# Attention stage of a fused kernel: a warm-up on the identity, gates behind the first maxima, one turning for the factors, the last x^T multiplied by VectorE, another tie rule for the plan

## The chip, the cores and the metric

The kernel runs on one core of one Trainium2 chip. The metric is device time in microseconds (us) of one execution; a kernel's time is the median of its runs. The engines are named as the profile names them: PE is TensorE (PEld its weight loads), DVE is VectorE, ACT is ScalarE, POOL is GpSimd and SP is SyncE, which here only issues DMAs. Each engine works through its own instructions in program order and waits for the others by semaphores.

## The reference: what is computed

Three layers follow each other: attention with a compressive memory, an expert layer with one expert (`_moe_ref`), and a gated layer with eight experts (`_moe2_ref`). The change lies in the first one alone.

```python
# q, k, v: (4, 8, 576, 64); M_prev: (4, 8, 64, 64); z_prev: (4, 8, 64); beta: (8,)
scores = scale * np.matmul(q, k.transpose(0, 1, 3, 2))
scores = np.where(causal, -1000000000.0, scores)
scores = scores - scores.max(-1, keepdims=True)
a = np.exp(scores)
a /= a.sum(-1, keepdims=True) + 1e-09
local = np.matmul(a, v)
q_p = phi(q)                                   # phi(x) = max(x, exp(x) - 1) + 1 by pieces
mem_ret = np.einsum('bhsd,bhde->bhse', q_p, M_prev)
mem_norm = np.einsum('bhsd,bhd->bhs', q_p, z_prev)[..., None] + 1e-06
g = 1.0 / (1.0 + np.exp(-beta))[None, :, None, None]
attn_out = g * (mem_ret / mem_norm) + (1 - g) * local
```

The layer behind it multiplies each token by `w_in` (512 x 2048), applies an elementwise function, and multiplies by `w_out`; the last one routes each token to one of eight experts.

## The kernel before, in words

**Stages.** `fused_kernel` calls `attention` and then `moe`. Attention works on 16 pairs of heads (`NPAIR`); beside it the same engines already convert `w_in` to two parts (`cv`, 16 pieces) and, from pair 13 on, split the first two blocks of x^T (`xs`). `moe` begins on PE with `gemm1` (L197 to L199: products of x and `w_in` into PSUM tiles `ph`), and `gemm2` (L249 to L251: into `py`) follows three steps behind it. The parts of `w_out` are made in `moe` itself, step by step (L800, L808, L813, L819, L829, L832).

**One pair.** Per pair p, with its two heads side by side:

- SP loads `qk` (q^T and k^T), `qn` (q by rows) and `vx` (M_prev and v). POOL scales q^T (`sq`, L1009). ACT, DVE, POOL and DVE make phi(q) and its sums with z_prev (`f1` to `f4`, L1012 to L1027; `f3` is L1022 and L1024).
- PE makes the scores of query tiles 0 to 4 (`S0` makes tiles 0 and 1 together, then `S2`, `S3`, `S4`; L1041 to L1049) into two PSUM tiles `ps`. DVE takes their maxima (`pk`, L1055 and L1058), ACT the exponents with their sums (`ex`, L1069).
- POOL and DVE work out the factors in two parts (`s0`, `s1`, `s2`: L1081, L1085, L1090, L1091), and POOL writes phi(q) times a factor in front of the exponents in `E` (`place0`, `place1`, L1095), so that one product gives both the memory part and the local part.
- PE turns the blocks of `E` (L1101, at most four blocks of 128 columns to a PSUM tile `pt`, of which there are two); DVE or ACT copies each `pt` to `eta` or `etb` (L1001 on DVE, L1003 on ACT) and so frees it. `AV0` and `AV1` (L1129) multiply `vx` with `eta` and `etb` into the one PSUM tile `px`.
- The normalising factors `rr` of the pair are turned as well (`r`: L1107 twice and L1108 once, into a `pt`), copied to `rt` in two copies (`re`), stored to DRAM in two DMAs (`rw`, L1117 and L1118) and read back spread over 64 partitions for each head (`rs`, L1122, two DMAs) as `R`.
- `xe` copies `px` to `xt` (`xr` for the last pair) on DVE or ACT, `X` multiplies it by `R` on POOL (L1141), and `xo` stores it (L1145).

**What sets the order.** Everything in attention between the constants and `moe` is a task of `Work`: a name, an engine (or "VA": DVE or ACT, whichever starts first), an assumed duration, a due time, and the names it depends on. `run` repeatedly takes the task with the smallest rank among those whose dependences are placed, assumes when it starts and ends, and at last writes all tasks in the order of their assumed starts. No hardware queue is reordered by it: the order in which the code is written is the program order of each engine. The rank before:

```python
start = max(ready, free[e])
rank = (round((start + turn) * 8), t[0], t[1])     # t[0]: due time, t[1]: number
```

Starts are compared in steps of an eighth of a microsecond, and within a step the earlier due time wins.

**Start and end of the stage.** Before the plan, DVE clears 512 columns of `E[1]` (L1259) and PE makes two products of these zeros into `px` (`keep_warm`, L1257). The gates (sigmoid of beta and what follows from it: L979 on ACT, `gates1` with L982 to L991 on DVE) depend on nothing but `beta`. At the end, `moe`'s first `ph` takes the PSUM banks that `px` had, and the first parts of `w_out` take the SBUF space that attention's tiles had, `R` among them.

## Time and profile before

| What | Value |
|---|---|
| time, median of 3 runs | 908.55 us (906.96 to 911.33) |
| the profiled execution | 907.34 us |
| its span | 905.6 us |
| PE busy | 840.3 us (93%), 5412 products |
| DVE busy | 579.4 us (64%) |
| ACT busy | 622.4 us (69%) |
| POOL busy | 288.2 us (32%) |

Attention takes the span from its start to 236.6 us, where PE begins with `ph`. Busy time is an average over stages: the share of PE over the whole span says little of attention, so the rows below take stretches of their own. A row of the timeline gives start, duration, engine, line, operation, the tiles written and read, the number of merged instructions, and in brackets how long the engine had been idle and what ended that. A "wait" row gives who waited for whom, the sum, the number of times and the longest.

### The profile page before, as it was taken

The page shows a single profiled execution, that of the slowest core. Times are in us where ns is not written, and L with a number is a line of the kernel's source. Part 1 is how long each engine was busy: PE and PEld are TensorE (multiplying, and loading weights), DVE is VectorE, ACT ScalarE, POOL GpSimd, SP SyncE. Part 2 cuts the span into 40 slices and gives each one's busy share as a digit, 9 for nine tenths or more (in the row PEclk, how much of TensorE's full clock was granted, in tenths as well). Part 3 has the DMA queues.
Part 4 walks back from the last instruction along what each step waited for, and adds up shares of the span by engine and source line. Part 5 has one row for each costly group of instructions (what it writes and reads, how often), then busy time and mean ns, then how long its engine had stood idle before and what let it go on. Part 6 is the DMA issues. An engine that isn't in the chain of part 4 may idle for free. (4 is left out here: it accounts for less than half of the span.)

```text
span 905.6 us, 15113 instructions
## 1 busy us (share of the span) xinstructions
PE 840.3 (93%) x5412; PEld 684.3 (76%) x5412; DVE 579.4 (64%) x1166; ACT 622.4 (69%) x1136; POOL 288.2 (32%) x363
## 2 busy tenths in 40 slices
PE   6889889999889999999999999999878989999995
PEld 3556556666779998989898989888856868778774
DVE  6988888766478843456575757575457765383661
ACT  4777668876488887787878787787754555373551
POOL 5875877754223230110101111111055212211200
PEclk8999999999999999999999999999999999999998
DMA  5666566642333231010101010122326968284610
GB/s 211 197 189 195 181 195 222 210 154 86 123 94 109 94 128 48 24 47 24 48 24 48 25 47 24 47 96 92 105 79 222 363 205 286 61 281 163 202 57 4
DMA packets 53704, 113.44 MB, mean 125 GB/s; under 512 B 12148, under 2 KB 17396, under 8 KB 53600
## 3 DMA queue, kind: packets, MB, share of 16 engines
q1 hardware_dynamic: 43968, 91.22, 31.0%
q0 software_dynamic: 4064, 10.42, 3.5%
q10 hardware_dynamic: 5568, 10.49, 3.2%
q8 instruction: 56, 0.92, 0.4%
q14 instruction: 48, 0.39, 0.1%
HBM read 94.47 MB, written 18.77 MB: 125 GB/s over the span
## 5 line engine op out<-in xcount | busy, mean ns | idle before, releaser
L197 PE MATMUL ph<-xh,u 128*128 128x256 f32 x576 | 163.8, 284 | 0.9 <-DVE xr L1001 0.9
L199 PE MATMUL ph<-xh,u 128*128 128x256 f32 x576 | 162.5, 282 | 0.0
L198 PE MATMUL ph<-xl,u 128*128 128x256 f32 x576 | 162.3, 282 | 0.0
L249 PE MATMUL py<-u,gh 128*128 128x512 f32 x288 | 115.2, 400 | 5.4 <-POOL u L832 5.1
L251 PE MATMUL py<-u,gl 128*128 128x512 f32 x288 | 114.5, 398 | 1.4 <-DVE gl L235 1.4
L250 PE MATMUL py<-u,gh 128*128 128x512 f32 x288 | 114.4, 397 | 0.0
L197 PEld LDWEIGHTS ph<-xh,u 128*128 128x128 f32 x576 | 109.8, 191 | 3.4 <-DVE xr L1001 1.1
L198 PEld LDWEIGHTS ph<-xl,u 128*128 128x128 f32 x576 | 109.9, 191 | 2.5
L199 PEld LDWEIGHTS ph<-xh,u 128*128 128x128 f32 x576 | 109.9, 191 | 0.0
L225 DVE SCALAR_TENSOR_TENSOR g<-t,g 128x512 f32<-128x512 f32 x72 | 49.9, 693 | 92.4 <-ACT t L221 92.4
L1069 ACT ACTIVATE e<-ps,nm 128x256 f32<-128x256 f32 (+4 forms) x144 | 77.9, 550 | 28.9 <-DVE nm L1058 21.4
L235 DVE TENSOR_TENSOR gl<-g,gh 128x512 fp32r<-128x512 f32 x72 | 51.9, 721 | 69.0 <-ACT gh L234 59.2
L1101 PE MATMUL pt<-ident,e 128*128 128x128 f32 x528 | 76.2, 282 | 10.3 <-ACT eta L1003 4.6
L351 POOL DMA_INDIRECT rt<-pay,sl x18 | 20.7, 1148 | 187.6 <-DVE pay L349 184.9
L209 ACT ACTIVATE g<-ph 128x512 f32<-128x512 f32 x72 | 42.7, 593 | 49.4 <-PE ph L199 47.6
L1101 PEld LDWEIGHTS pt<-ident,e 128*128 128x128 f32 x528 | 56.6, 141 | 20.6 <-ACT eta L1003 6.4
L106 POOL TENSOR_TENSOR xl<-xr,xh 128x256 fp32r<-128x256 f32 x36 | 31.5, 880 | 112.0 <-ACT xh L105 111.8
L249 PEld LDWEIGHTS py<-u,gh 128*128 128x128 f32 x288 | 54.8, 190 | 16.0 <-POOL u L832 5.3
L251 PEld LDWEIGHTS py<-u,gl 128*128 128x128 f32 x288 | 54.4, 189 | 15.7 <-DVE gl L235 2.5
L832 POOL TENSOR_TENSOR u<-cvf,u 128x512 fp32r<-128x512 f32 x32 | 46.6, 1456 | 58.1 <-ACT u L829 58.1
L250 PEld LDWEIGHTS py<-u,gh 128*128 128x128 f32 x288 | 54.6, 189 | 9.8
L1058 DVE TENSOR_REDUCE nm<-ps 128x2 f32<-128x256 f32 (+1 forms) x64 | 51.3, 816 | 9.2 <-PE ps L1049 8.2
(238 smaller groups left out, 1987.3 us busy)
## 6 DMA issues: line engine op xcount, KB each, us to landing
raw<-w SPq DMA_DIRECT2D x25, 512.0 KB
qk<-qk SPq DMA_DIRECT2D x16, 608.0 KB
raw<-w_in SPq DMA_DIRECT2D x16, 512.0 KB
raw<-w_out SPq DMA_DIRECT2D x16, 512.0 KB
xl<-w SPq DMA_DIRECT2D x16, 512.0 KB
xh<-w SPq DMA_DIRECT2D x15, 512.0 KB
qn<-qn SPq DMA_DIRECT2D x16, 384.0 KB
vx<-vx SPq DMA_DIRECT2D x16, 320.0 KB
```

Of the source, the lines that this page charges most:

```text
L197: T.matmul(ps[:, f2], win(HI, k, f), hi[:, k], start=(k == 0), stop=False)
L198: T.matmul(ps[:, f2], win(HI, k, f), lo[:, k], start=False, stop=False)
L199: T.matmul(ps[:, f2], win(LO, k, f), hi[:, k], start=False, stop=(k == KD - 1))
L225: V.scalar_tensor_tensor(out=g, in0=t, scalar=ROOT_HALF, in1=g, op0=ALU.add, op1=ALU.mult)
L235: V.tensor_tensor(out=gl, in0=g, in1=gh.bitcast(F32), op=ALU.subtract)
L249: T.matmul(ys[i][t], gh[:, f2, ts], wout(HI, f), start=(f == 0), stop=False)
L250: T.matmul(ys[i][t], gh[:, f2, ts], wout(LO, f), start=False, stop=False)
L251: T.matmul(ys[i][t], gl[:, f2, ts], wout(HI, f), start=False, stop=(f == KF - 1))
L832: self.nc.gpsimd.tensor_tensor(out=lo, in0=self.now.pop(i), in1=hi.bitcast(F32), op=ALU.subtract)
L1058: V.tensor_reduce(out=nm, in_=ps[:, :, o:o + w], axis=AX.X, op=ALU.max, negate=True)
L1069: A.activation(out=E[p % 2][:, k, 64:64 + w], in_=src, func=AF.Exp, bias=nm[:, h:h + 1], scale=1.0, accum_out=SS[p % 2][:, 0, k:k + 1])
L1101: T.transpose(ps[:, c], E[p % 2][:, k, j * 128:(j + 1) * 128], ident)
```

## The change

Five edits, all in attention and in the planner:

- The warm-up products are twelve products of the identity with itself, 128 columns each, put ahead of the first loads; the two on zeros and the clearing for them are gone.
- The gates get due times and dependences: ACT's part waits for the first `f1`, DVE's part for the third maxima of pair 0 (`(0, "pk", 2)`, which are tile 2's). Two tasks stand for the loads of pair 0, so that the plan knows when they land; `load(0, "vx")` now comes first of the planned loads.
- The factors `rr` (nine columns) are turned by one transpose, copied by one copy and stored by one DMA. Reading them back takes four DMAs (per head one for the full tiles in pieces of 128 values, one for the 64 values of the last tile) in place of two. The due times of `r`, `re` and `rw` are 1.3 us, 1.3 us and 1.2 us earlier.
- The last pair's `px` is multiplied by `R` on DVE, straight from PSUM, in place of a copy on DVE and a product on POOL. It so depends on `rs` of that pair.
- The rank of the plan is the start plus a twentieth of the due time, unrounded.

```diff
-                        rank = (round((start + turn) * 8), t[0], t[1])
+                        rank = (start + turn + 0.05 * t[0], t[0], t[1])
...
+        for i in range(12):
+            T.matmul(px[:, 0, 0:128], ident, ident, start=True, stop=True)
         load(0, "qk")
         load(0, "qn")
...
         def turn_r(p):
             pts[p, "r"] = ps = ps_t.tile([128, 4, 128], F32, name="pt")
-            r = rrs.pop(p)[:, 0]
+            T.transpose(ps[0:NS, 0], rrs[p][:, 0], ident)
+
+        def keep_r(e, p):
+            evac(e, rt_, pts.pop((p, "r"))[0:NS, 0])
+
+        def store_r(p):
+            SP.dma_start(out=rd[p % 2], in_=rt_)
+
+        def spread_r(p):
+            d = rd[p % 2]
             for h in range(2):
-                T.transpose(ps[0:NQT, h], r[:, h:2 * NQT:2], ident)
-            T.transpose(ps[0:1, 2], r[:, 2 * NQT:NS], ident)
...
+                SP.dma_start(out=R[p % 2][HS[h], 0:QW].rearrange("p (t q) -> p t q", t=NQT),
+                             in_=d[0:2 * NQT].rearrange("(t h) (a q) -> h a t q", h=2, a=1)[h].to_broadcast([64, NQT, 128]))
+                SP.dma_start(out=R[p % 2][HS[h], QW:S], in_=d[2 * NQT:NS, HS[h]].to_broadcast([64, 64]))
...
-            evac(e, xt, pxf[:, 256:256 + S])
+            if p < NPAIR - 1:
+                evac(e, xt, pxf[:, 256:256 + S])
+            else:
+                V.tensor_tensor(out=xt, in0=pxf[:, 256:256 + S], in1=R[p % 2], op=ALU.mult)
...
-        wk.add(("lv0",), "S", 0.5, 0.5, lambda: load(0, "vx"), lag=3.5)
-        wk.add(("g0",), "A", 0.25, 4.0, gates0)
-        wk.add(("g1",), "V", 2.1, 5.0, gates1, [("g0",)])
+        wk.add((0, "lq"), "S", 0.5, -30.0, lambda: load(0, "vx"), lag=4.5)
+        wk.add((0, "ld"), "G", 0.1, -30.0, lambda: None, lag=4.0)
+        wk.add(("g0",), "A", 0.25, 4.0, gates0, [(0, "f1")])
+        wk.add(("g1",), "V", 3.0, 7.0, gates1, [("g0",), (0, "pk", 2)])
...
-            wk.add(key("r"), "T", 0.35, o + P + 3.3, lambda p=p: turn_r(p), [key("s2", 0), key("s2", 1)], take="t")
+            wk.add(key("r"), "T", 0.15, o + P + 2.0, lambda p=p: turn_r(p), [key("s2", 0), key("s2", 1)], take="t")
...
+            end = p == NPAIR - 1
+            wk.add(key("xe"), "V" if end else "VA", {"V": 0.7, "A": 0.6}, o + P + 8.0, lambda e, p=p: out_x(e, p),
+                   [key("AV0"), key("AV1")] + [("xs", 1, KD - 1), key("rs")] * end + [prev2("xo")])
...
-        V.memset(wtile[:, 0:512], 0.0)
-        for _ in range(2):
-            keep_warm()
         wk.run()
```

What that does to the order of the engines, at three places. The names in the rows: `nm` are negated maxima, `mn` is phi(q) on its way, `ss` are sums, `by` the gates by query tile; `eta`, `etb`, `pt`, `px`, `ps` as above.

DVE at the start of the stage, before (the last two copies, L990 and L991, come twice):

```order
L982 TENSOR_SCALAR gates<-gates 128x12
L983 RECIPROCAL gates<-gates 128x12
L984 TENSOR_SCALAR gates<-gates 128x12
L985 TENSOR_SCALAR gates<-gates 128x12
L986 RECIPROCAL gates<-gates 128x12
L987 TENSOR_TENSOR gates<-gates 128x12
L990 COPY by<-gates 128x4x2 x4
L991 COPY by<-gates 128x4
L1058 TENSOR_REDUCE nm_245<-ps 128x2
L1058 TENSOR_REDUCE nm_247<-ps 128x2
```

The same place on DVE with the change (its lines are two further down):

```order
L1019 SCALAR_TENSOR_TENSOR qn<-qn,mn_120 128x576
L1060 TENSOR_REDUCE nm_239<-ps 128x2
L1060 TENSOR_REDUCE nm_243<-ps 128x2
L1060 TENSOR_REDUCE nm_247<-ps 128x2
L1029 TENSOR_REDUCE ss_124<-mn_120 128x9
L984 TENSOR_SCALAR gates<-gates 128x12
L985 RECIPROCAL gates<-gates 128x12
L986 TENSOR_SCALAR gates<-gates 128x12
L987 TENSOR_SCALAR gates<-gates 128x12
L988 RECIPROCAL gates<-gates 128x12
L989 TENSOR_TENSOR gates<-gates 128x12
L992 COPY by<-gates 128x4x2 x4
```

The gates moved from ahead of the maxima of pair 0 to behind its first three maxima and `f4`; the fourth maxima (tile 3) come right behind them.

PE in the middle of the stage, around the turning of the factors of pair 7, before:

```order
L1101 MATMUL pt<-ident,e_114 128x128 x8
L1129 MATMUL px<-eta,vx 64x256 x2
L1129 MATMUL px<-eta,vx 64x192 x2
L1129 MATMUL px<-eta,vx 64x64 x2
L1101 MATMUL pt<-ident,e_114 128x128 x8
L1041 MATMUL ps<-qk 128x512
L1041 MATMUL ps<-qk 128x64
L1042 LDWEIGHTS idb
L1042 MATMUL ps<-m_138,idb 128x64
L1101 MATMUL pt<-ident,e_114 128x128 x3
L1107 MATMUL pt<-ident,rr 4x128 x2
L1108 MATMUL pt<-ident,rr 1x128
```

PE with the change, around the turning of the factors of pair 8:

```order
L1103 MATMUL pt<-ident,e_113 128x128 x8
L1127 MATMUL px<-eta,vx 64x256 x2
L1127 MATMUL px<-eta,vx 64x192 x2
L1127 MATMUL px<-eta,vx 64x64 x2
L1103 MATMUL pt<-ident,e_113 128x128 x4
L1107 MATMUL pt<-ident,rr 9x128
L1048 MATMUL ps<-qk 128x512 x2
```

The turning of the factors stood at the end of the pair's turnings; it now stands further ahead, in front of a score step. Over the whole stage, turnings of `E` with nothing but the factors' turning between them make 11 runs of 11 or more before and 3 with the change; the rest are runs of 8 or fewer.

PE at the passage from attention to `moe`, before:

```order
L1101 MATMUL pt<-ident,e_114 128x128 x15
L1107 MATMUL pt<-ident,rr 4x128 x2
L1108 MATMUL pt<-ident,rr 1x128
L1129 MATMUL px<-etb,vx 64x320 x6
L1129 MATMUL px<-etb,vx 64x256 x2
L1129 MATMUL px<-etb,vx 64x128 x2
L197 MATMUL ph<-xh,u_86 128x256
```

And with the change:

```order
L1103 MATMUL pt<-ident,e_114 128x128 x8
L1107 MATMUL pt<-ident,rr 9x128
L1103 MATMUL pt<-ident,e_114 128x128 x7
L1127 MATMUL px<-etb,vx 64x320 x6
L1127 MATMUL px<-etb,vx 64x256 x2
L1127 MATMUL px<-etb,vx 64x128 x2
L197 MATMUL ph<-xh,u_86 128x256
```

The last pair's factors are turned seven turnings earlier. From L197 on, PE's and SP's instructions are the same in both.

## Rows read from the trace of the kernel before

**Rows 1.** Three stretches: start and end, length, busy us (count) by engine, PEclk.

```profile
30.00:236.00 206.00, 186.75 (x1579) 125.08 (x1576) 164.62 (x274) 148.74 (x423) 138.16 (x210) 1.00 0.55 174
253.40:256.40 3.00, 2.94 (x7) 2.35 (x8) 2.93 (x4) 2.98 (x5) 1.64 (x1) 0.50 0.20 81
300.00:600.00 300.00, 299.38 (x1935) 269.22 (x1935) 174.66 (x470) 241.09 (x363) 45.15 (x45) 1.00 0.14 46
```

**Rows 2.** Waits of 30 to 236 us: who waited for whom, us, times, longest.

```profile
POOL xt L1141 <- DMA r<-rd: 22.3, 9, 5.4
...
PE pt L1107 <- DVE etb L1001: 5.5, 6, 1.2
...
PE pt L1101 <- ACT eta L1003: 4.3, 7, 1.6
...
PE pt L1101 <- POOL e L1095: 2.3, 2, 2.0
...
PE pt L1107 <- ACT etb L1003: 2.2, 2, 1.2
PE pt L1101 <- DVE etb L1001: 2.2, 3, 1.5
```

**Rows 3.** Timeline of the first 22 us: start, us, engine, line, operation, tiles.

```profile
1.10 0.29 POOL masks.py:199 TENSOR_SCALAR_AFFINE_SELECT ident<-ident 128x128 f32<-128x128 f32 x1
...
5.01 0.88 POOL L1009 TENSOR_SCALAR qk<-qk,nums,one 128x640 f32<-128x640 f32 x1 [1.04 <-DMA qk<-qk]
...
5.80 3.78 PE L1257 MATMUL px<-e 128*128 128x512 f32 x4 [5.80 <-DVE e L1259]
...
7.90 0.17 DVE L982 TENSOR_SCALAR gates<-gates 128x12 f32<-128x12 f32 x1
...
9.51 0.80 PE L1046 MATMUL ps<-qk 64*128 64x128 f32 x4
...
11.55 0.16 DVE L991 COPY by<-gates 128x4 f32<-128x4 f32 x1
11.62 1.01 DVE L1058 TENSOR_REDUCE nm<-ps 128x2 f32<-128x256 f32 x2
...
14.51 2.08 PE L1046 MATMUL ps<-qk 64*128 64x512 f32 x4 [2.42 <-DVE cvf L808]
...
18.81 1.72 POOL L1022 TENSOR_TENSOR mn<-qn 128x512 f32<-128x512 f32 x1 [1.65 <-DVE qn L1017]
...
19.08 1.12 PE L1101 MATMUL pt<-ident,e 128*128 128x128 f32 x4
...
21.22 0.21 POOL L1090 TENSOR_TENSOR rr<-rr,by 128x12 f32<-128x12 f32 x1
```

**Rows 4.** Groups of 30 to 225 us by shape: count, busy us, mean ns.

```profile
L1003 ACT ACTIVATE rt<-pt 4x256 f32<-4x256 f32 x11 | 4.0, 367 | 2.7 <-PE pt L1108 2.7
...
L1003 ACT ACTIVATE rt<-pt 1x128 f32<-1x128 f32 x11 | 2.8, 250 | 0.0
```

**Rows 5.** Timeline of the passage from attention to `moe`, 232 to 254 us.

```profile
232.83 0.38 PE L1107 MATMUL pt<-ident,rr 128*4 128x128 f32 x2 [0.58 <-DVE etb L1001]
...
233.35 0.61 DVE L1001 COPY rt<-pt 4x256 f32<-4x256 f32 x2 [0.30 <-PE pt L1108]
...
235.75 1.11 SPq L1122 DMA_DIRECT2D r<-rd  x2
235.78 0.76 DVE L1001 COPY xr<-px 128x576 f32<-128x576 f32 x1 [1.82 <-PE px L1129]
...
236.59 0.39 PE L197 MATMUL ph<-xh,u 128*128 128x256 f32 x1 [0.86 <-DVE xr L1001]
...
239.60 1.43 POOL L1141 TENSOR_TENSOR xr<-xr,r 128x576 f32<-128x576 f32 x1 [8.07 <-DMA r<-rd]
241.06 0.63 ACT L829 ACTIVATE u<-cvf 128x512 fp32r<-128x512 f32 x1 [7.04 <-POOL xr L1141]
...
253.45 0.76 PE L249 MATMUL py<-u,gh 128*128 128x512 f32 x1 [5.09 <-POOL u L832]
```

## The prediction, made before the change was run

> **What bounds the kernel now.** I read the stretches first. From 300 to 600 us PE is busy 299.38 us of 300 [rows 1]: behind attention the program is bound by PE's own products, and its order from the first `ph` on is unchanged. So a microsecond by which PE reaches `ph` earlier or later is a microsecond of the whole, and nothing else in the change can count. From 30 to 236 us PE is busy 186.75 us of 206, DVE 164.62, ACT 148.74 and POOL 138.16 [rows 1]: PE is the fullest engine of attention as well, but it stands idle for 19.25 us. The waits say for what: five rows of PE's waits add up to 5.5 + 4.3 + 2.3 + 2.2 + 2.2 = 16.5 us, and every one of them is a turning into `pt` (L1101, L1107) that waits for DVE or ACT to copy an earlier `pt` away, or for POOL to fill `E` [rows 2]. So attention has three prices to look at: PE's own work, these 16.5 us, and the start and the end of the stage, which I read from the timeline [rows 3, 5].

> The sum is made against the profiled execution, 907.34 us (span 905.6 and 1.74 around it). The median of the runs is 1.2 us above it.

> **Warm-up.** The first score product starts at 9.51, when the two products of zeros end (5.80 + 3.78 = 9.58); its operand has been ready since 5.01 + 0.88 = 5.89 [rows 3]. The identity is there at 1.10 + 0.29 = 1.39, so the twelve new products can start then. They are 24 instructions in the trace's way of counting, where two products of zeros were 4. Their price has two bounds. A quarter of a 512-column one: 3.78 / 4 / 4 = 0.236 us, 24 of them 5.7 us, ending at 7.1. Or a turning of 128 columns as at 19.08: 1.12 / 4 = 0.28 us, in all 6.7 us, ending at 8.1 [rows 3]. I take 7.4, near the first since it is the same kind of product: the scores start 2.1 us earlier (1.4 to 2.4, and 3.6 if the products ran so fast that the operand decides).

> **Gates.** DVE works on them from 7.90 to 11.55 + 0.16 = 11.71 and takes the first maxima at 11.62, though the first score block ended at 9.51 + 0.80 = 10.31 [rows 3]. Without that, and with scores 2.1 us earlier, the maxima can come at about 8.3, 3.3 us earlier, and so can ACT's exponents and the second PSUM tile, for which PE's next scores waited 2.42 us up to 14.51 [rows 3]. Not all of it stays: the same 3.81 us of gates now stand on DVE ahead of the fourth maxima, and behind those wait the fourth exponents and the reciprocal of pair 0. I count 2.5 us for warm-up and gates together (0 to 4).

> **Pair 0's factors.** On POOL, `f3` of pair 1 (L1022, 18.81 for 1.72 us, and its small second half) stood ahead of the factors of pair 0 (L1090 at 21.22) [rows 3]; with the change it comes behind them, so they can come up to 2.4 us earlier. `place0` and pair 0's turnings hang on them; behind them other copies are late next. I count 1.5 (0 to 2.4). That `vx` of pair 0 is loaded ahead of `qk` and `qn` of pair 1 shifts those by one issue on SP, and POOL has `f3` of pair 0 before it needs them: nothing. Start in all: -4.0 (0 to -6.4).

> **Turning the factors.** PE makes one transpose in place of three per pair; two of L1107 took 0.38 us where one takes 0.27, so a step is 0.11 us [rows 5], two steps less 0.22 us, 16 pairs 3.5 us. PE is busy nine tenths of the stage, and where it then waits the gain is lost: -2.5 (0 to -3.5). The copies of 367 and 250 ns become one of about 250 [rows 4]; neither engine is full, so this only frees `pt` 0.37 us sooner and belongs to the waits. On SP one store replaces two, and four reads two: 1.11 us of issue [rows 5] becomes about 2.2 per pair, so `R` is complete up to 1.1 us later after the first read. Behind the reads on SP stand loads for later pairs and stores of x^T, which have slack; behind POOL's product with `R` stand the next pair's factors and `place`, and POOL waited for `R` 9 times, 22.3 us in all [rows 2]. That the factors are now turned ahead of one or two score steps, and not right ahead of `AV1`, gives `R` some 2 to 3 us of lead. I set both against each other, at nothing.

> **The new order.** This is the largest unknown: the planner's choices move nearly every task. What I can read from the order is that turnings come in 3 long runs in place of 11. With two `pt` of four blocks, a run of 8 only needs the buffers that are there, and each four blocks beyond it wait for a copy that was only just made possible. That is what the 4.3 + 2.2 us of L1101 behind DVE and ACT show, and the 7.7 us of L1107, which stood at the end of such a run [rows 2]. From below, none of the 16.5 us goes and new waits of 3 us come; from above, 12 of them go. I take -4.5, about a quarter: the copies themselves remain, on engines that also have maxima and exponents to do.

> **The passage to `moe`.** Before, `px` is free at 235.78 + 0.76, and PE begins after 0.86 us of idling; `R` was only needed by POOL at 239.60 [rows 5]. Now `px` is free when DVE has multiplied, and that needs `R`. From the start of the last factors' turning to `R` it was 239.60 - 232.83 = 6.8 us. One copy and one store fewer take some 0.6 off, two more reads add up to 1.1: 6.2 to 7.3. PE meanwhile has seven turnings (about 1.0, and a wait or two) and `AV1`, which with the rest of the factors' turning took from 232.83 to 235.78, and so some 4 us in all. So `R` is 2.2 to 3.3 us late, the multiplication takes as long as the copy, and PE waits that much longer: +2.6. Something comes back. ACT's first part of `w_out` overwrites `R`'s place and waited for POOL's product until 241.06, which is 4.47 us after `ph` began; the activations of the first blocks queued behind it on ACT, and `gemm2` waited 5.09 us up to 253.45 [rows 5]. Now that wait ends when `ph` begins. The activations can't start before their products are there, so not all of the 4.47 comes back: -2.0 (0 to -4.4).

> [...]

> Passage: +2.6 - 2.0 + 0.4 = +1.0 (-3.7 to +4.8).

> **Sum.** -4.0 - 2.5 - 4.5 + 1.0 = -10.0: the profiled execution would take 897.3, and the median, 1.2 above, **898.5 us**.

> **Rivals.** [...] (2) *`R` takes back what the order gives*: reads in smaller pieces, four of them, land later, and POOL waits longer in front of the next pair's `place`, for which PE then waits. At 1.1 us in each of the 9 pairs that waited, it takes 9.9 us from POOL; if PE feels three quarters of it, the gain shrinks by 7.5: 906. For it speaks that this queue exists (22.3 us, [rows 2]); against it that PE's waits for POOL came to 2.3 us alone. (3) *Slower: the factors' early turning blocks a buffer.* It takes one of two `pt` in the middle of a pair, and its copy stands on ACT or DVE behind exponents or maxima of up to about 1 us; PE then waits for `pt` at the next turning of every pair. At 1.1 us for each of 16 pairs this adds 17.6 us in place of the 4.5 gained: 898.5 + 4.5 + 17.6 = 920.6. It decides from 0.63 us per pair on: then the waits cost 10.0 us, the other terms give 5.5, and the kernel is 4.5 us, or 0.5%, slower. Against it: before, the turning stood right in front of `AV1`, and waited 7.7 us already [rows 2]. (4) *The change does nothing*: start and waits are covered by something else that is late next, and only PE's own 2.5 us remain against the passage: 907.

> **How the numbers follow.** Forecast (a gain of 6 to 16 us): 0.70. Rival 1: 0.11. Rival 2: 0.08. Rival 3: 0.05. Rival 4: 0.06. About 0.5%, 4.5 us, is what a measurement of this kernel can tell from no change: faster is below 904.0, slower above 913.1. The forecast and rival 1 lie below, rivals 2 and 4 in between, rival 3 above: 0.81, 0.14, 0.05. The bounds of the terms add up to -25.6 and +7.8; all at one end is unlikely. The range goes down to 891.0, a gain of 17.5, where half of the 16.5 us went and the start gave its full 6.4, and up to 906.0, which takes in rival 1 and rival 2. Outside are rivals 3 and 4 and the far ends of the forecast, together below 2 in 10.

> **What would show each step.** The first score product at 7 to 8 us, the first maxima right behind it, and `AV1` of pair 0 some 4 us earlier: start right. One transpose of `rr` per pair and PE's busy time in attention 3 us less: turning right. The waits of L1101 and of the factors' turning well below 16.5 us in sum: order right; above it, rival 3. POOL's wait for `R` far above 22.3 us, and PE's for POOL with it: rival 2. At the passage, an idle time before `ph` of 3 to 4 us and one before `gemm2` of about 3; if the first is over 5, the passage is mis-sized. The prediction is wrong as a whole if PE reaches `ph` later than about 231 us.

## The result, and the profile after

The changed kernel takes **910.76 us** (median, 906.01 to 914.89), the kernel before 906.25 us beside it: a ratio of 1.0051 with a 95% interval of 1.0035 to 1.0068. It is slower by half a percent, where the prediction said 898.5 us and faster. The profiled execution is 911.03 us, its span 909.2.

Three stretches tell where the time went. They are read from the first and last start of PE's products of line L197, the first line of `gemm1`, and from the span. First the kernel before, then the changed one (duration least, median and most in ns, then first and last start):

```profile
core 0 of [0], span 905.6 us
...
L197 PE MATMUL ph<-xh,u x576: 277/283/387, 236.6 to 653.0; 128*128 128x256 f32 x192
```

```profile
core 0 of [0], span 909.2 us
...
L197 PE MATMUL ph<-xh,u x576: 274/283/415, 227.9 to 645.4; 128*128 128x256 f32 x192
```

| Stretch | before | changed | difference |
|---|---|---|---|
| start to first `ph` | 236.6 | 227.9 | -8.7 |
| first `ph` to last product of L197 | 416.4 | 417.5 | +1.1 |
| last product of L197 to the end | 252.6 | 263.8 | +11.2 |

Attention did what the sum said (8.4 us for everything ahead of `ph`). The loss is in the stage in which each token goes to its expert, hundreds of microseconds behind the change, in code that the change doesn't touch. PE's waits there, from 690 us on, before (first fence) and changed:

```profile
PE ph L495 <- PEq L761: 7.1, 7, 2.4
PE py L505 <- DVE h0l L483: 1.3, 1, 1.3
```

```profile
PE ph L495 <- issue: 7.1, 1, 7.1
PE ph L495 <- PEq L761: 4.5, 6, 1.9
PE ph L496 <- issue: 3.8, 2, 2.9
PE py L505 <- DVE h0l L483: 1.0, 1, 1.0
PE py L479 <- DMA y<-yd,ids: 0.7, 1, 0.7
PE ph L497 <- issue: 0.7, 1, 0.7
```

L761 is the branch that leaves out blocks of an expert which has few tokens; PEq is PE's sequencer. What is new is "issue", 7.1 + 3.8 + 0.7 = 11.6 us in which PE waited for nothing that the profile shows. The timeline of PE at the first and the second of these places:

```profile
736.62 1.08 PE L505 MATMUL py<-u,h1l 128*128 128x512 f32 x4
744.80 0.79 PE L495 MATMUL ph<-u,ah 128*128 128x512 f32 x1 [7.10 <-issue]
...
800.92 0.47 PE L495 MATMUL ph<-u,ah 128*128 128x512 f32 x1 [1.88 <-PEq L761]
...
801.69 0.39 PE L495 MATMUL ph<-u,ah 128*128 128x512 f32 x1
805.01 0.79 PE L496 MATMUL ph<-u,ah 128*128 128x512 f32 x1 [2.93 <-issue]
805.60 0.63 PE L497 MATMUL ph<-u,al 128*128 128x512 f32 x1
```

At 800.92 PE resumes behind a branch, runs four products, and stands again. Behind both pauses a product takes 0.63 us and not 0.40, and the next one starts after 0.43 us and not 0.23: the granted clock has fallen to 0.50 (half clock, in what follows). Four stretches of the changed kernel at this level, two at the passage to `moe` and two here (start and end, length, PE busy with products and their count, clock, share of the DMA engines, GB/s):

```profile
228.70:232.00 3.30, 3.30 (x17) 0.50 0.81 255
245.80:249.10 3.30, 3.30 (x10) 0.50 0.20 25
740.70:750.90 10.20, 6.10 (x14) 0.50 0.69 229
802.20:808.80 6.60, 3.79 (x9) 0.50 0.87 283
```

The last two hold 6.10 + 3.79 = 9.9 us of work at half clock. But the kernel before has such stretches behind the same two branches as well:

```profile
748.00:751.40 3.40, 3.40 (x10) 0.50 0.96 308
802.60:806.00 3.40, 3.40 (x10) 0.50 0.86 275
```

So 3.1 us of work at half clock are new. Half of that, 1.5 us, is my estimate of their cost, from the clock of 0.50. The rows of PE's waits add up to 8.4 us before and to 17.8 us changed, 9.4 us more (one of the seven waits for L761 is now part of the 7.1 us). Together that is 10.9 of the 11.2 us.

### The profile page after: what moved, and what is told of

It reads as the page before. It is cut to its first block, busy times and chain, and to the rows that moved or that the text cites. A ratio compares the mean times of both kernels' runs of the same rounds, so it can differ in the third digit from the quotient of the medians.

```text
span 909.2 us, 15077 instructions
## 1 busy us (share of the span) xinstructions
PE 847.1 (93%) x5400; PEld 690.3 (76%) x5400; DVE 577.7 (64%) x1161; ACT 619.6 (68%) x1124; POOL 285.6 (31%) x362
## 4 chain that ended last, share of the span: by engine, by line
PE 56%; DMA 14%; issue 13%; POOL 5%; DVE 5%; ACT 4%; SPq 1%; POOLq 0%; another core or an unknown queue 0%; DVEq 0%; ACTq 0%
DMA cvt<-yd,ids 8%; PE ph L197 8%; PE ph L199 7%; PE ph L198 7%; PE py L249 7%; PE py L251 7%; PE py L250 7%; PE pt L1103 4%; DMA out<-cvf,ids 3%; PE px L1127 3%; PE ps L1048 3%; DMA qn<-qn 1%; DVE nm L1060 1%; PE ps L1043 1%; POOL u L462 1%
## 5 line engine op out<-in xcount | busy, mean ns | idle before, releaser
L197 PE MATMUL ph<-xh,u 128*128 128x256 f32 x576 | 165.2, 287 | 3.0 <-DVE xr L1137 3.0
L197 PEld LDWEIGHTS ph<-xh,u 128*128 128x128 f32 x576 | 111.4, 193 | 5.6 <-DVE xr L1137 3.3
L199 PEld LDWEIGHTS ph<-xh,u 128*128 128x128 f32 x576 | 111.2, 193 | 0.0
L1071 ACT ACTIVATE e<-ps,nm 128x128 f32<-128x128 f32 (+2 forms) x144 | 78.0, 552 | 19.5 <-DVE nm L1060 10.8
L499 ACT ACTIVATE h<-ph 128x512 f32<-128x512 f32 x32 | 19.0, 595 | 64.6 <-PE ph L497 59.8
```

The costliest lines, as they stand in the source:

```text
L197: T.matmul(ps[:, f2], win(HI, k, f), hi[:, k], start=(k == 0), stop=False)
L199: T.matmul(ps[:, f2], win(LO, k, f), hi[:, k], start=False, stop=(k == KD - 1))
L1071: A.activation(out=E[p % 2][:, k, 64:64 + w], in_=src, func=AF.Exp, bias=nm[:, h:h + 1], scale=1.0, accum_out=SS[p % 2][:, 0, k:k + 1])
```

## The experiments

Three theories. **A, code layout**: PE's program is 37 instructions shorter in front of the expert stage (9,296 where it was 9,333, counted from the program's first instruction), so its branches stand elsewhere against the pieces in which its code is loaded. The changed kernel's page lists queue q8, "instruction", with 58 packets and 0.95 MB: 16 KB each, and from 21 to 695 us the trace has one for 256 PE instructions on average. **B, time shift**: the expert stage begins 8 us earlier and meets other transfers. **C**: chance of the single execution. (The expectations also give the length as 9,302, 9,265 and 9,303: those are PE's rows in the trace ahead of the first of these branches. The count from the first instruction is 31 higher in each kernel, and modulo 256 they use that one. No row shows the 31; only differences of places are used below.)

This table has all fourteen runs. "Place" is the number of PE instructions in front of the nested branches, modulo 256; "end" is the stretch from the last product of L197 to the end of the span; "issue" is the longest such wait of PE behind 690 us (a dash: none over 0.5 us). Times are those of each kernel's profiled execution, but for the median.

| Kernel | place | first `ph` | first `py` | end | issue | median |
|---|---|---|---|---|---|---|
| before | 117 | 236.6 | 253.5 | 252.6 | - | 906.25 |
| changed | 80 | 227.9 | 244.7 | 263.8 | 7.1 | 910.76 |
| pa19 | 118 | 227.8 | 245.8 | 247.9 | - | 898.67 |
| pa64 | 208 | 229.8 | 246.5 | 252.0 | - | 899.15 |
| pa9 | 98 | 227.0 | 243.7 | 259.6 | 3.3 | 907.69 |
| pa128 | 80 | 228.1 | 244.8 | 260.3 | 6.2 | 911.85 |
| pb110 | 81 | 234.5 | 251.1 | 257.4 | 3.3 | 911.85 |
| oldrule | 85 | 243.6 | 260.3 | 257.4 | 3.7 | 920.96 |
| newrule | 93 | 226.4 | 243.2 | 259.1 | 2.3 | 904.34 |
| nostart | 42 | 226.1 | 241.3 | 252.7 | - | 896.43 (one run) |
| noturn | 135 | 230.2 | 247.8 | 253.4 | - | 903.39 (one run) |
| nolastx | 80 | 225.0 | 240.4 | 265.9 | 8.0 | 908.55 (one run) |
| rankturn | 42 | 225.4 | 240.6 | 251.7 | - | 894.17 |
| rankturn19 | 80 | 224.8 | 240.2 | 265.2 | 6.7 | 907.64 |
| nolastx19 | 118 | 226.7 | 242.1 | 252.3 | - | 896.47 |
| exfirst | 118 | 224.9 | 240.4 | 248.9 | - | 896.05 |

### Where the branches stand: pa19, pb110, pa64

The edit is the same in all: products of one zero with one zero, early, where PE waits for its first data. In pa19 there are 19 and in pa64 64 of them in the changed kernel, in pb110 110 in the kernel before, ahead of its loads. The clearing of the two zeros is one more instruction on DVE in every kernel that has them, with and without a loss.

```diff
+        zb = c1.tile([128, 2], BF16, name="zb")
+        V.memset(zb, 0.0)
+        for _ in range(19):
+            T.matmul(px[0:1, 0, 0:1], zb[:, 0:1], zb[:, 1:2], start=True, stop=True)
         for i in range(12):
             T.matmul(px[:, 0, 0:128], ident, ident, start=True, stop=True)
```

> The changed kernel with 19 products of one zero with one zero (1x1, 38 PE instructions by the trace's way of counting) ahead of the warm-up; nothing behind them is touched. With them PE's program is as long in front of the expert stage as before the change (9303 instructions against 9302 before and 9265 changed). Theory A, code layout: the gain of attention is lost in the expert stage only because PE's branches there now stand differently against the pieces in which its code is loaded. Then the stretch from the last gated-layer product (`ph` of L197's stage) to the end takes about 188 us again in place of 199, the 7.1 us wait of `ph L495` for `issue` is gone, and the median is about 898 to 900. Theory B, time shift: the expert stage meets other transfers because it begins 8 us earlier, whatever the layout: the stretch stays near 199 us and the median near 911. Theory C, a chance of each execution (the clock's phase): the stretch differs from run to run, and the median lies in between with a spread over 1%.

> The kernel before with 110 products of one zero with one zero (220 PE instructions by the trace's way of counting) in front of the first loads, where PE is idle until 5.8 us. This moves PE's program against its code pieces to about where the changed kernel has it (81 in place of 80, counted modulo 256), and leaves the times of attention as they were (first `ph` near 236.6). Theory A, code layout: the expert stage takes about 199 us in place of 188 and the median is about 917. Theory B, time shift: nothing changes, 906. Theory C: 906 with a wide spread.

> The changed kernel with 64 products of one zero with one zero (128 PE instructions) ahead of the warm-up: a third place of the branches against the code pieces (208 modulo 256). Theory A: a third time for the stage behind the gated layer, between 188 and 199 us or beyond, that differs from the changed kernel's by more than 2 us, with another list of waits of `ph L495` and `L496`; which one, the theory does not say. Theory B: 199 us as in the changed kernel, 911.

pa19: 898.67 us, ratio 0.9922 (0.9893 to 0.9952). Attention ends where it did (`ph` at 227.8), and the end of the kernel takes 247.9 us in place of 263.8. PE's waits from 690 us on:

```profile
PE ph L495 <- PEq L761: 6.0, 7, 2.2
PE py L505 <- DVE h0l L483: 0.8, 1, 0.8
```

No "issue" is left. Nineteen products that compute nothing make the kernel 12 us faster. pa64: 899.15 us, ratio 0.9932 (0.9902 to 0.9961), again without "issue". In pb110 the same products make the kernel *before* slower, 911.85 us, ratio 1.0056 (1.0035 to 1.0078), though its attention ended 2 us earlier; the size was missed, since only 5 of the 11 us appeared (3.3 us of "issue" at one place in place of 7.1); why, the next part tells. B expected no difference from any of these and falls. C falls too: the interval of none touches that of its parent. A holds.

### The period, and a pair: pa128, pa9, rankturn, rankturn19

rankturn is the changed kernel with the old start (warm-up on zeros, gates at once) and the old last x^T; the new rank and the single turning of the factors stay. It came out of the attributions below. rankturn19 puts the 19 products into it. pa9 and pa128 are 9 and 128 products in the changed kernel.

```diff
-        for i in range(12):
-            T.matmul(px[:, 0, 0:128], ident, ident, start=True, stop=True)
...
-        wk.add(("g0",), "A", 0.25, 4.0, gates0, [(0, "f1")])
-        wk.add(("g1",), "V", 3.0, 7.0, gates1, [("g0",), (0, "pk", 2)])
+        wk.add(("g0",), "A", 0.25, 4.0, gates0)
+        wk.add(("g1",), "V", 2.1, 5.0, gates1, [("g0",)])
...
-            end = p == NPAIR - 1
+            end = False
```

> The changed kernel without the two edits that cost time in the runs so far: the old start (warm-up on zeros, gates at once; 1.8 us earlier `ph` by itself) and the last pair's x^T by a copy and POOL (4.3 us earlier `py` by itself). If the two add up, the first `py` is at 244.7 - 3.4 - 4.3 = 237.0. PE's program stands at 42 modulo 256, where the kernel with the old start took 252.7 us from the last `ph` of L197 to the end. So theory A expects 894.6 - 4.3 = 890 for the span and a median near 892. If the edits do not add up (the plan falls out otherwise), `py` is at 240 to 241 and the median at 896.

> The same with the 19 products of one zero with one zero ahead of the first loads, which cured the changed kernel. Here they take PE's program from 42 to 80 modulo 256, where the changed kernel and the one without the x^T edit stand. Theory A, code layout modulo 256: the stage from the last `ph` of L197 to the end takes 260 to 266 us in place of about 252, PE waits 6 to 8 us for `issue` at one `ph L495`, and the median is 8 to 14 us above the kernel without the products. If the products did good for another reason (theory A wrong), the two medians agree within 2 us.

> The changed kernel with 128 such products ahead of the warm-up, 256 PE instructions: its layout is 80 modulo 256 again, as without any. Theory A with a period of 256 instructions: the stage from the last `ph` of L197 to the end is 257 to 266 us, PE waits for `issue`, and the median is 910 to 914 (the start may come up to 2 us later). If the loss came from the number of products and not from the place of the branches, it goes away as with 19 and 64 of them: 248 to 253 us and 898 to 900.

> The changed kernel with nine such products ahead of the warm-up: 98 modulo 256, between the slow places (80 to 93) and the fast ones (117 and 118). Theory A: the stage from the last `ph` of L197 to the end lies between 248 and 260 us, with fewer or shorter waits for `issue` than the 11.6 us of the changed kernel; the theory does not say where between. Theory B (time shift): 264 us as in the changed kernel, 911.

rankturn is the fastest of all by its median: 894.17 us, ratio 0.9841 (0.9813 to 0.9868). Its `py` is at 240.6, so the two edits that it takes out do not add up. With the products that cured the changed kernel it takes 907.64 us, ratio 0.9995 (0.9968 to 1.0022): its attention is as early as before them (`ph` at 224.8 and 225.4), and 13.5 us are lost behind it. This is the same edit with the other sign, as the place says (42 to 80). rankturn19's waits from 690 us on, and PE at the first branch in rankturn19 and in rankturn:

```profile
PE ph L495 <- issue: 6.7, 1, 6.7
PE ph L495 <- PEq L761: 5.6, 6, 2.3
PE ph L496 <- issue: 2.7, 2, 2.4
```

```profile
735.52 1.08 PE L505 MATMUL py<-u,h1l 128*128 128x512 f32 x4
743.26 0.79 PE L495 MATMUL ph<-u,ah 128*128 128x512 f32 x1 [6.66 <-issue]
```

```profile
732.61 1.08 PE L505 MATMUL py<-u,h1l 128*128 128x512 f32 x4
735.35 0.47 PE L495 MATMUL ph<-u,ah 128*128 128x512 f32 x1 [1.66 <-PEq L761]
```

The queue of PE's code at these places (packets, MB, share of 16 engines), in rankturn19 from 733 to 743.3 and from 740.9 to 742 us, and in rankturn from 732 to 736:

```profile
q8 instruction: 2, 0.03, 1.2%
```

```profile
q8 instruction: 1, 0.02, 5.6%
```

```profile
q8 instruction: 1, 0.02, 1.5%
```

In rankturn one packet is loaded, from 732.75 to 733.74, and PE resumes 1.6 us later. In rankturn19 there are two, one behind the other: 735.44 to 736.40 and 740.94 to 741.92, and PE resumes 1.3 us behind the second. The changed kernel (736.52 to 737.79 and 741.15 to 743.49, PE at 744.80) and pa128 (736.69 to 737.73 and 741.41 to 742.38, PE at 743.72) show the same pair. So this skip went with one load of code and 1.66 us in rankturn, and with two in a row and 6.66, 7.10 and 6.19 us in the other three. My reading is that in these the target stands right in front of the edge of a piece, so that the next piece is needed at once, and that the four products between the two waits at 801 us stood ahead of such an edge: in the changed kernel one load ends at 799.34, and the next runs from 802.76 to 803.90 us.

PE's rows, counted from the first of the nested branches on, agree with it. Between the two loads of the changed kernel stands one row, the `EVENT_SEMAPHORE` of L761 on which the skip lands, at 739.3 us and row 287; row 288, PE's first weight load for `ph`, comes at 744.79, behind the second load. All second pauses of over 1.5 us, those that begin behind a landing and have a load of code in them, come 1 to 13 rows behind one of four landings (rows 287, 800, 1,434 and 1,570):

| Place | rows of the second pauses | place + row |
|---|---|---|
| 80 (four kernels) | 288, 809 | 368, 889 |
| 81 (pb110) | 808 | 889 |
| 85 (oldrule) | 804, 1,447 | 889, 1,532 |
| 93 (newrule) | 1,439, 1,578 | 1,532, 1,671 |
| 98 (pa9) | 1,435, 1,573 | 1,533, 1,671 |

For each instruction more ahead the pause comes one row earlier, in one case to within a row, as the edge of a piece would. By the same reading pb110 lost only half because at 81 the edge of the first pause, 368 - 81, falls on row 287, the landing itself, and the first load brings what follows as well: PE waits 2.27 us for L761 there, with no "issue" behind it. What the sequencer did between the landing and the second load (from 739.3 to 741.15 in the changed kernel) no row shows.

pa128 has the 256 extra instructions that bring the place back to 80, and the loss is back: 911.85 us, ratio 1.0040 (1.0020 to 1.0060), "issue" 6.2 us. With pa64 at 208 being fast (899.15 us), these runs agree with a period of 256 and not with one of 128. pa9, at 98, is still slow: 907.69, ratio 1.0014 (0.9991 to 1.0037). All kernels at 42, 117, 118, 135 and 208 took 247.9 to 253.4 us for the end, all at 80 to 98 took 257.4 to 265.9. Other places were not tried.

### What the parts of attention were worth: oldrule, newrule, nostart, noturn, nolastx

Each takes one edit out of the changed kernel, but for newrule, which is the kernel before with the new rank alone. They are judged by the first `ph` and `py`, because each has a place of its own. Five kernels with the very order of the changed one (it, pa9, pa19, pa64, pa128) spread from 227.0 to 229.8 in `ph`, mean 228.1, and two with that of before lie 2.1 us apart: below 2 us nothing is told.

```diff
-                        rank = (start + turn + 0.05 * t[0], t[0], t[1])
+                        rank = (round((start + turn) * 8), t[0], t[1])
```

> The changed kernel with the old rank in the planner (start rounded to an eighth, then due time); all other edits stay. Judged by the start of the first `ph` (236.6 before, 227.9 changed), since the expert stage may have a layout of its own. By the prediction's sum the new rank was worth 4.5 us: `ph` at 232.4. Rival: the rank matters little beside the start, the turning of factors and the gates, `ph` at 228 to 229. Other rival: the whole gain needs the new rank, `ph` at 236 or later.

> The kernel before with the new rank alone (start plus a twentieth of the due time, unrounded). Judged by the start of the first `ph` (before 236.6, changed 227.9, changed with the old rank 243.6). If the rank is worth its 15.7 us by itself, `ph` is at 221 and the other edits cost 7 us; if the two only work together, as I expect, `ph` comes between 229 and 236 and PE's waits for `pt` fall from 16 us to under 10. The code layout theory leaves the stage behind it open: PE's program is 93 modulo 256 here, beside 80 to 85 of the three slow ones (257 to 264 us from the last `ph` of L197 to the end) and 117, 118 and 208 of the three others (248 to 253).

oldrule, the diff above: `ph` at 243.6, and 920.96 us, ratio 1.0169 (1.0141 to 1.0198). newrule, the reverse in the kernel before: `ph` at 226.4, -10.2 us (-8.1 against pb110, which has the order of before), and 904.34 us, ratio 0.9982 (0.9960 to 1.0003), at a slow place. PE's waits for `pt` in newrule from 30 to 236 us, the longest three of five:

```profile
PE pt L1101 <- ACT eta L1003: 1.2, 2, 0.8
PE pt L1101 <- DVE etb L1001: 1.0, 3, 0.4
PE pt L1101 <- POOL e L1095: 0.9, 1, 0.9
```

In all 4.2 us are left of the 16.5 [rows 2], or of 17.2 with a sixth row of 0.7 that the prediction left out. My expectation that the rank needs the other edits was wrong: it brings its gain by itself, and the other four together bring none. With them but the old rank, the plan is 7 us worse than before.

nostart takes out the new warm-up and gates, as in rankturn's diff; noturn puts the three transposes, two copies, two stores and two reads back; nolastx the copy and POOL's product of the last pair.

> The changed kernel with the old start: two products of zeros for the warm-up, gates without dependences and with their old due times and durations. All else stays changed. The prediction's terms for warm-up and gates were 2.5 us: first `ph` at 230.4 in place of 227.9. Rival: the start is covered by what is late next, `ph` within 1 us of 227.9. Other rival: the plan falls out differently as a whole, `ph` off by over 5 us with other waits. Layout 42 modulo 256: the stage from the last `ph` of L197 to the end below 255 us if only 80 to 93 is bad.

> The changed kernel with the factors turned as before (three transposes, two copies, two stores, two reads, with their old due times). The prediction's term was 2.5 us of PE: first `ph` at 230.4. Rival: the four reads cost POOL and PE what the transposes give, `ph` at 227.9 or earlier. Layout 135 modulo 256: the stage from the last `ph` of L197 to the end below 255 us.

> The changed kernel with the last pair's x^T copied and then multiplied by POOL, as for the other pairs. The prediction's terms: PE's idle time before the first `ph` falls from 3.0 to about 0.9 (`ph` 2 us earlier), and the one before `gemm2` grows from 3.5 to about 5, so that the first `py` is near the changed kernel's 244.7, within 1.5 us. PE's program has the same number of instructions as in the changed kernel, so by the code layout theory the stage from the last `ph` of L197 to the end stays slow: above 257 us, time near 911.

nostart: `ph` at 226.1, no later than with the new start. noturn: `ph` at 230.2, 2.1 us behind the mean of the five; that agrees with the 2.5 of the sum and is hardly above the spread. PE's own work tells more: from 30 us to `ph` it is busy 187.6 us in noturn and 184.6 to 186.0 in the five, 2.2 us less on average. nolastx: `ph` at 225.0 and `py` at 240.4, where the five have 228.1 and 245.1; by this kernel the edit costs 3.1 us at `ph` and 4.7 at `py`. The second was a miss: I had expected `gemm2` to take most of it back. Other kernels put it lower: nolastx19 below, with the same order as nolastx, is at 226.7 and 242.1 (1.4 and 3.0), and with the old start it is 0.7 at both (rankturn against nostart). The end of nolastx, at place 80, stayed slow (265.9), as expected.

### Where the start's gain went: exfirst, nolastx19

```diff
-            wk.add(key("f1"), "A", 1.2, q0 + 1.5, lambda p=p: phi1(p), [key("lq"), prev2("f4")])
+            wk.add(key("f1"), "A", 1.2, q0 + 1.5, lambda p=p: phi1(p), [key("lq"), prev2("f4")] + [(0, "ex", 2, 1)] * (p == 1))
```

> The changed kernel with the last x^T by a copy and POOL, the 19 products of one zero with one zero ahead of the warm-up (118 modulo 256), and one more dependence: ACT's `f1` of pair 1 behind the third pair of exponents of pair 0. In the order only this differs from the next kernel: two instructions of `f1` on ACT stand behind six exponents in place of ahead of them. If the start's gain is lost because these exponents stand behind `f1` of pair 1, which waits for its `qn` until 11.1 us, then the first exponents come at about 9.0 in place of 12.4, the scores of the second `ps` at 10.5 to 11.5 in place of 14.2, and the first `ph` 2 to 3.5 us earlier than in the next kernel. Rival: what is late next (POOL's `place0` behind `f3`, the loads of pair 1) covers it, and the first `ph` agrees within 1 us although the scores come earlier.

> The changed kernel with the last x^T by a copy and POOL and the 19 products of one zero with one zero: 118 in place of 80 modulo 256. Control of the kernel above. Theory A, code layout: first `ph` near 225 as without the products, but the stage from the last `ph` of L197 to the end at 248 to 253 us in place of 265.9, and a median of 894 to 896 in place of 908.6.

Both are nolastx with the 19 products; exfirst has the diff above as well. The timeline of the control, nolastx19, and of exfirst:

```profile
11.70 0.68 ACT L1018 ACTIVATE mn<-qn 128x576 f32<-128x576 f32 x1 [3.98 <-DMA qn<-qn]
13.01 0.35 ACT L1075 ACTIVATE e<-ps,nm 128x128 f32<-128x128 f32 x1
...
14.76 2.08 PE L1052 MATMUL ps<-qk 64*128 64x512 f32 x4 [6.39 <-ACT e L1075]
```

```profile
9.71 0.37 ACT L1075 ACTIVATE e<-ps,nm 128x128 f32<-128x128 f32 x1 [2.29 <-DVE nm L1064]
...
11.48 1.13 PE L1052 MATMUL ps<-qk 64*128 64x512 f32 x4 [2.12 <-ACT e L1075]
12.42 0.71 ACT L1018 ACTIVATE mn<-qn 128x576 f32<-128x576 f32 x1
```

In the control ACT stands 3.98 us in front of pair 1's phi, whose `qn` is on its way, with the exponents of pair 0 behind it in the queue. With the two exchanged, exponents and second scores come 3.3 us earlier. Of that, 1.5 us are left at `AV1` of pair 0 (28.57 and 30.05) and 1.8 at `ph` (224.9 and 226.7), less than was expected, more than its rival allowed, and within the spread; the medians, 896.05 (890.20 to 900.69) and 896.47, don't differ. nolastx19 itself is the second pair of the layout test: 896.47 in place of 908.55, and its end 252.3 in place of 265.9.

## Why the prediction was wrong

**The premise failed, not the sum.** The step was: "a microsecond by which PE reaches `ph` earlier or later is a microsecond of the whole, and nothing else in the change can count", since the order from the first `ph` on is unchanged. It was read from 300 to 600 us, where PE is busy 299.38 of 300 [rows 1]; from 653.0 us to the end PE is busy 225.2 of 252.6 in the kernel before, and waits for L761 stood there already, 7.1 us. The order was unchanged, but not the place of the code: the warm-up, the turnings and the new order changed the number of PE's instructions, and the end of this kernel, which has branches, changed with it: 263.8 us at place 80, 247.9 at 118 (pa19). With the place put back near the old one (pa19) the changed kernel takes 898.67 us, against the 898.5 that the sum gave; without it, the stage behind takes 11.2 us more than before and the gain is gone. None of the rivals had it: they were about attention and its passage.

The prediction gave these branches no term. In the kernels without "issue" one skip cost up to 3.1 us (nostart); at place 80 the place of the target made 6.2 to 8.0 us of it.

That 228 us for the first `ph` were right is partly luck, since the terms were not:

- *Start, -4.0*: the first scores came at 6.86 and the first maxima at 8.11, where 7.4 and 8.3 were expected. But ACT's exponents came at 12.44 (before: 12.73), behind pair 1's phi, and PE's next scores at 14.20 in place of 14.51 [rows 3]:

```profile
6.86 0.49 PE L1048 MATMUL ps<-qk 64*128 64x128 f32 x4
...
8.11 1.89 DVE L1060 TENSOR_REDUCE nm<-ps 128x2 f32<-128x256 f32 x3 [0.17 <-PE ps L1051]
11.14 0.68 ACT L1014 ACTIVATE mn<-qn 128x576 f32<-128x576 f32 x1 [3.90 <-DMA qn<-qn]
12.44 0.35 ACT L1071 ACTIVATE e<-ps,nm 128x128 f32<-128x128 f32 x1
14.20 2.08 PE L1048 MATMUL ps<-qk 64*128 64x512 f32 x4 [5.32 <-ACT e L1071]
```

  The failing step is "and so can ACT's exponents": what stands ahead of them in ACT's queue wasn't read. `AV1` of pair 0 did come 3.4 us earlier, but it does so with the old start as well (29.63 and 29.38). At `ph` the edit is worth nothing (nostart); exfirst gets half of it back as far as `AV1`.
- *Turning, -2.5*: 2.1 by noturn, and 2.2 of PE's busy time; right as far as the spread tells.
- *New order, -4.5*: it is -10.2 by newrule, or -8.1 against pb110. The mechanism was right, runs of turnings that waited for their `pt`; but more than two thirds of the 16.5 us went (4.9 are left in the changed kernel), where a quarter was assumed, on the ground that the copies remain. They do, but in time.
- *Passage, +1.0*: PE's idle time ahead of `ph` is 3.02 us, and 0.86 in nolastx, so `R` costs 2.2 us there, near the +2.6. In all it is 3.1 us at `ph` and 4.7 at `py` by nolastx, near the upper bound of +4.8, but 1.4 and 3.0 by nolastx19: above the +1.0, and not told more closely.

The passage of the changed kernel, to be held against [rows 5]:

```profile
220.37 0.27 PE L1107 MATMUL pt<-ident,rr 128*9 128x128 f32 x1 [0.44 <-DVE etb L1003]
...
224.16 0.61 SPq L1120 DMA_DIRECT2D r<-rd  x1
227.13 0.76 DVE L1137 TENSOR_TENSOR xr<-px,r 128x576 f32<-128x576 f32 x1 [4.75 <-DMA r<-rd]
227.95 0.38 PE L197 MATMUL ph<-xh,u 128*128 128x256 f32 x1 [3.02 <-DVE xr L1137]
```

From the factors' turning to `R` are 6.8 us, within the 6.2 to 7.3; PE idles 3.02, within the 3 to 4; `gemm2` waits 3.5 in place of 5.1. But in nolastx, where POOL still holds the place of `w_out`, it waits only 3.7, and 3.5 in rankturn: what came back of the -2.0 comes without this edit too. No run shows the +0.4 that the passage's sum adds, which was meant for the clock. In its place half clock followed both pauses, at 228.7 and at 245.8 in the stretches above, where before there was one such piece, behind the wait of 5.09 us [rows 1, 5]: 6.6 us of work in place of 2.94. Half of the difference, 1.8 us, is my estimate of the cost, from the clock of 0.50. But in nostart none follows its pause of 2.91 us ahead of `ph` at 226.1, while pa9's pause of 2.89 us ahead of its `ph` is followed by 3.4 us of it, and pa64 has none behind its 3.46 us ahead of `py`, where the changed kernel has one behind the same 3.46: the pause alone doesn't decide. What does is open. The stretch behind nostart's pause:

```profile
226.00:232.00 6.00, 5.91 (x49) 1.00 0.72 217
```

*Rivals 2 to 4*: POOL's wait for `R` fell from 22.3 us [rows 2] to 2.3, and PE's waits for `pt` from 16.5 to 4.9, so neither the reads nor the early turning of the factors took anything back. POOL and PE (the two longest of five rows for `pt`) in the changed kernel, from 30 to 236 us:

```profile
POOL xt L1142 <- DMA r<-rd: 2.3, 4, 1.2
```

```profile
PE pt L1103 <- DVE eta L1003: 1.8, 4, 0.8
PE pt L1107 <- DVE etb L1003: 1.3, 3, 0.7
```

One sum of the prediction doesn't come out, and nothing hangs on it: the lower end of the range, 891.0, is put down to half of the 16.5 us and 6.4 for the start; with -2.5 and +1.0 these make a gain of 16.2 us and not 17.5.

What stays open: why the second pause one row behind a landing takes 4.5 to 5.5 us at the first skip and 2.8 at another (pa9); why one kernel at 80 loses 8 us at its end against before (pa128) and others 11 to 13; and why nostart and nolastx, each good for some 2 to 5 us at `py`, are not better together (rankturn's `py` at 240.6).

## What to carry to other kernels

- An edit that only changes the number of instructions gave or cost more than 1% here, in a later stage that has branches (ratio 0.9922 for pa19, where the changed kernel has 1.0051; 0.9995 for rankturn19, where rankturn has 0.9841). Where a kernel's time doesn't move with the stage that was changed, compare the stages of both traces from a common landmark, and look for "issue" behind branches; then try the same kernel with a few idle instructions ahead before the edit is judged. A result at one place is not the edit's worth.
- Where a planner lays out a pipeline, its tie rule can be worth more than all edits of the work itself, and they must be tried apart: here rank alone -8 to -10 us at `ph`, the four other edits nothing in sum.
- A gain at one engine's first task can end at the next engine's queue: the first scores came 2.65 us earlier here, ACT's exponents behind pair 1's phi 0.29. Read what stands ahead of the task that is to profit.

## What was unexpected of the hardware

```profile
735.00:755.00 20.00, 12.90 (x49) 0.74 0.71 233
```

```profile
735.00:755.00 20.00, 19.39 (x94) 1.00 0.89 302
```
